# Two borders and one tick order: a long convolution with a spectral mix, its stages between batch pairs put in another order

## The chip, the cores and the metric

The kernel runs on one core of a Trainium2 chip. The metric is the device time of one execution in microseconds (us). TensorE (PE) multiplies matrices into the accumulator memory PSUM, VectorE (DVE) and ScalarE (ACT) copy results out of PSUM into the on-chip memory SBUF and do the elementwise work, GpSimd (POOL) and SyncE (SP) here mostly issue DMA transfers. Each engine works through its own list of instructions in order, and engines wait for one another by semaphores.

## The reference

An input x of 8 batches, 5696 positions and 128 channels is convolved causally with a filter h of 5696 positions, by Fourier transforms of twice the length. The result goes through a spectral mix of its lowest 64 modes and a small dense layer:

```python
Yf = np.fft.rfft(x, n=L, axis=1) * np.fft.rfft(h, n=L, axis=0)[None]   # L = 2 * S
v = np.fft.irfft(Yf, n=L, axis=1)[:, :S, :]
X = np.fft.rfft(v, axis=1)                          # modes 0..63 are mixed
Yr = einsum(Xr, w_r) - einsum(Xi, w_i)              # 'bmd,mde->bme'
Yi = einsum(Xr, w_i) + einsum(Xi, w_r)
u = v + np.fft.irfft(Y, n=S, axis=1)                # Y is zero above mode 63
out = u + np.maximum(u @ w_ch, 0.0)
```

## The kernel before

The 5696 positions are split as 89 times 64. The batches are worked on in four pairs (`for g_ in range(NP)`, L682), numbered 0 to 3 here. For each pair there are two parts.

The first transform runs over the 89. `a_tile(j, slots, eng)` (L438) makes one of 32 tiles of it: four matmuls of 180 columns with constant `F` (in SBUF `Xin` holds the pair's input), into a slot of two PSUM banks, and one eviction to `As` with a scale, on ACT or DVE. Tile 31 is evicted in two halves, one on each engine ("both"). Slots are named by their first bank: 0, 2, 4, 6.

Then come 23 ticks (`NT`), one for each group of four of the 90 frequencies (the last has two). In tick t of a pair, `tick(g_, t)` (L612) issues:

- the placing of a piece of the next pair's input into `Xin` on DVE, in eight of the ticks (`x_place`, L355, by the list `XPLACE`);
- the second transform of group t (`second`, L568): 16 matmuls whose operands `As` and `M` have 64 rows, into slot 0 or 2;
- its product with the filter's spectrum (`products`, L579): ACT copies the slot to `Xs`, DVE multiplies `Xs` with `Hs` into `U`;
- a load of the next pair's input by POOL (`x_load`);
- the third transform of group t - 2 (L634 to L649): two halves of two matmuls of 512 columns on `U`, each into one of the banks 4, 5, 6 in turn, evicted by ACT to `Zs` (or `Zt`), then written to DRAM (`zscr`) by a DMA that SP issues;
- the mode sums of group t - 3 (L655 to L668): eight matmuls of `Zs` with `G`, all added up in bank 7 over the whole pair;
- in ticks 0 to 16 of pair 0 only, a filter group (`filter_tick`, L455): 16 matmuls of 64 rows on `Ah` into banks 2 and 3, evicted by DVE to `Hs`, and two DMAs by SP that copy it across partitions. It is for the product six ticks later.

In the pairs 1 to 3, two second transforms are issued together in every other tick. In pair 0, while there is filter work, second transforms have only slot 0. There the kernel before issues second(t + 1) already in tick t, from tick 2 on, between the third transform and the mode sums:

```python
if g_ == 0 and LC <= t < NT - 1:
    second(g_, t + 1)
```

As third transform and mode sums lag by two and three ticks, ticks 23 to 25 only finish them. After the last pair they run as they are; after pairs 0, 1 and 2 the first six tiles of the next pair's first transform are put among them by a list `border` (L521) of tile, slot and engine:

```python
border = {NT - 1: [(0, 0, V)], NT: [(1, 2, V), (2, 0, V)],
          NT + 1: [(3, 2, A), (4, 0, V)], NT + 2: [(5, 2, V)]}
```

Then ACT copies the mode sums out of bank 7 (to `XT`), and the other 26 tiles follow in four slots, on ACT and DVE in turn with two on ACT in a row every ninth (L696). `keep(n, b0)` (L537) issues n matmuls of constants into banks b0 and b0 + 1 whose results nobody reads. In the borders POOL also issues pieces of a rewriting of the mixing weights to DRAM, one after every other tile.

After the four pairs come the mix of the modes, the inverse transform from `zscr`, the dense layer and the output; the change does not touch them.

`share(n)` (L428) chooses between ACT and DVE for an eviction: it adds a given cost to each engine's running sum and takes the smaller. The kernel before uses it for the first pair's first transform only.

Of the kernel before, what the change touches and what calls it, by code (L numbers as in the profile page):

```python
# [123 lines left out]
def bass_long_conv_fft__then__afno_spectral_mix_kernel(nc, x, h, moe_w_r, moe_w_i, moe_w_ch, out):  # L124
# [8 lines left out]
    NP = B // 2  # L133
# [103 lines left out]
    XC = 4  # L237
# [117 lines left out]
    def x_place(i, src, toks):  # L355
        R.add("vector", lambda e: e.tensor_copy(bass.AP(x_sb, i * XN * XS, [[XW, NQ], [XS, XN], [1, D]]),  # L356
                                                bass.AP(src, 0, [[XB, NQ], [D, XN], [1, D]])),
              list(toks) + XZ, [("xin", i)])
# [159 lines left out]
            [("s4", part, 0)], after=pace + (AST if part else M_ALL[1:4]))  # L518

    V, A = "vector", "scalar"  # L520
    border = {NT - 1: [(0, 0, V)], NT: [(1, 2, V), (2, 0, V)], NT + 1: [(3, 2, A), (4, 0, V)], NT + 2: [(5, 2, V)]}  # L521
    early = {0: lambda: load_id(), 1: lambda: load_w(0), 3: lambda: load_w(1), 6: lambda: load_w(2), 8: lambda: load_w(3),
             12: lambda: load_s4(1), 16: lambda: load_s4(0),
             14: lambda: clear_zt(0),
# [20 lines left out]
    def with_h_at(g_, t):  # L545
        return g_ == 0 and t + LH < NT
# [10 lines left out]
    def twin(g_, t):  # L557
        return g_ > 0 and t % 2 == 1

    def straight(g_, t):  # L560
        return g_ > 0 and t % 4 == 3
# [6 lines left out]
    def second(g_, t):  # L568
        sl = slot_of(g_, t)
        for i, k in enumerate(ticks[t]):  # L570
            for r in range(2):
                for b in range(2):
                    col = k * 3 * J + (J if r == 0 else 0) + b * J
                    mm(pv(sl + b, i * D, [[1, D]]),
                       ap(m_sb, MW, J * b, J, col, [[1, P]]),
                       ap(a_sb, AW, J * b, J, (2 * k + r) * D, [[1, D]]), r == 0, r == 1,
                       AST + mtok(k), [bank(sl + b)])

    def products(g_, t, sl):  # L579
        n = len(ticks[t])  # L580
        bk = [bank(sl), bank(sl + 1)]
        i = t % NU
        hv = bass.AP(h_sb, KT * t * D, [[2 * HW, P], [HW, 2], [0, 2], [1, n * D]])
        uv = bass.AP(u_s[i], 0, [[2048, P], [1024, 2], [512, 2], [1, n * D]])
        src = pv(sl, 0, [[0, 2], [512, 2], [1, n * D]])
        if t == 0:
            e = turns("e", list(range(NXS)))
            evac(bass.AP(x_s[e], 512, [[1024, P], [1, n * D]]), pv(sl + 1, 0, [[1, n * D]]), [bank(sl + 1)], [("xs", e)], eng="scalar")
            hv = bass.AP(h_sb, 0, [[2 * HW, P], [HW, 2], [1, n * D]])
            for b, s_, tok, done in ((0, pv(sl, 0, [[0, 2], [1, n * D]]), bank(sl), ("u", i)),  # L590
                                     (1, bass.AP(x_s[e], 512, [[1024, P], [0, 2], [1, n * D]]), ("xs", e), ("u0", i))):
                R.add("vector", lambda e, b=b, s_=s_: e.tensor_tensor(bass.AP(u_s[i], b * 512, [[2048, P], [1024, 2], [1, n * D]]), s_, hv, MULT),  # L592
                      [tok, ("h", t, 0), ("h", t, 1, 0), ("h", t, 1, J)], [done])
            return
        if not straight(g_, t):
            e = onchip.get((g_, t))
            if e is None:
                e = copied(g_, t, sl)
            src, bk = bass.AP(x_s[e], 0, [[1024, P], [0, 2], [512, 2], [1, n * D]]), [("xs", e)]
        R.add("vector", lambda e: e.tensor_tensor(uv, src, hv, MULT),  # L600
              bk + [("h", t, 0), ("h", t, 1, 0), ("h", t, 1, J)], [("u", i)])
# [7 lines left out]
    def xtok(n):  # L609
        return [("xt", n, p_) for p_ in range(2)]  # L610

    def tick(g_, t):  # L612
        if g_ + 1 < NP:
            for i in range(2 * XC):
                if t == XPLACE[g_ > 0][i]:
                    x_place(i, x_st[i], xtok(i))
        with_h = with_h_at(g_, t)
        if t < NT:
            of_two = t > 0 and twin(g_, t - 1)
            if not of_two and not (g_ == 0 and t > LC):  # L620
                second(g_, t)
            products(g_, t, slot_of(g_, t))
            if twin(g_, t):
                second(g_, t + 1)
                if straight(g_, t):
                    copied(g_, t + 1, slot_of(g_, t + 1))
        drain = list(border[t]) if t in border and g_ + 1 < NP else []
        if drain and t >= NT:
            j, sl, e = drain.pop(0)
            a_tile(j, [sl], e)  # L630
        if g_ + 1 < NP and t % 2 == 0 and 0 < t <= 4 * XC:
            i = t // 2 - 1
            x_load(g_ + 1, i, x_st[i], xtok(i), [("u", t % NU)] + AST)
        if LC <= t < NT + LC:  # L634
            s_ = t - LC
            n = len(ticks[s_])
            i, zi = s_ % NU, zroom(g_, s_)
            zb = [turns("z", ZBANK) for b in range(2)]
            for b in range(2):
                for r in range(2):  # L640
                    mm(pv(zb[b], 0, [[1, n * D]]), (W1, W2)[r], u_s[i][:, r * 1024 + b * 512:r * 1024 + b * 512 + n * D],
                       r == 0, r == 1, [("u", i), ("wc",)] + ([("u0", i)] if s_ == 0 and b else []), [bank(zb[b])])
                evac(bass.AP(z_s[zi], b * D, [[1024, P], [2 * D, n], [1, D]]),
                     pv(zb[b], 0, [[D, n], [1, D]]), [bank(zb[b])], [("zs", zi, b)], eng="scalar",
                     after=once(("zx", zi, b), Z_OLD) if zi >= NZ else ())
            zo = (g_ * NK + KT * s_) * P * 256
            dma("sync", bass.AP(zs, zo, [[256, P], [P * 256, n], [1, 256]]),
                bass.AP(z_s[zi], 0, [[1024, P], [256, n], [1, 256]]), "z",
                [("zs", zi, 0), ("zs", zi, 1)], [("zd", g_, s_)])  # L649
            if drain and t >= NT:  # L650
                j, sl, e = drain.pop(0)
                a_tile(j, [sl], e)
        if g_ == 0 and LC <= t < NT - 1:
            second(g_, t + 1)
        if LM <= t < NT + LM:  # L655
            s_ = t - LM
            zi = zroom(g_, s_)
            for b in range(2):
                for i, k in sorted(enumerate(ticks[s_]), key=lambda q: (s_ > 0 or q[1] != 1, q)):
                    if k % 2:  # L660
                        o, off, n, sl = pv(MB, b * P, [[1, P]]), (k + 1) // 2 * P, P, (k + 1) // 2
                    else:
                        ms, off = even[k]
                        n, sl = 2 * len(ms), 0
                        dims = [[M, 2]] if len(ms) == 1 else [[ms[1] - ms[0], 2], [M, 2]]
                        o = pv(MB, b * P + ms[0], dims)
                    mm(o, z_s[zi][:, i * 256 + b * P:i * 256 + b * P + P], g_sb[:, off:off + n],
                       k == 1 and b == 0, k == NK - 1 and b == 1, [("g", sl // GP), ("zs", zi, b)], [bank(MB)])  # L668
        if drain and t < NT + LM - 1:
            j, sl, e = drain.pop(0)  # L670
            a_tile(j, [sl], e)
        if with_h:
            filter_tick(t + LH, [2, 3])

# [5 lines left out]
            filter_tick((j - 11) // 3, [b_, b_ + 1], share(512))  # L680
    keep(12, turns("s", SLOTS))
    for g_ in range(NP):  # L682
        for t in range(NT + LM):
            tick(g_, t)
            if g_ == 0 and t < 2:
                keep(8, 4)
            assert g_ + 1 < NP or not wp
            if g_ == NP - 1 and t in early:
                pace[:] = [("u", min(t, NT - 1) % NU)]
                early[t]()  # L690
        evac(bass.AP(xt, 2 * g_ * XTW + M, [[B * XTW, P], [XTW, 2], [1, P]]), pv(MB, 0, [[P, 2], [1, P]]),
             [bank(MB)], [("xt", g_)], 1.0 / 64, eng="scalar", after=[("ag", k) for k in range(NS + 2 * XN, NK)])
        evac(bass.AP(xt, 2 * g_ * XTW, [[B * XTW, P], [XTW, 2], [1, M]]), pv(MB, M, [[P, 2], [1, M]]),
             [bank(MB)], [("xtn", g_)], -1.0 / 64, eng="vector" if g_ + 1 == NP else "scalar", after=[("ag", k) for k in range(NS + 2 * XN, NK)])
        if g_ + 1 < NP:
            for j in range(6, 32):  # L696
                a_tile(j, [(4, 6, 0, 2)[(j - 7) % 4] if j > 6 else 0], "both" if j == 31 else (A, V)[(j - 6) % 9 % 2])
                if j == 31:
                    keep(8, 6)
                if wp and j % 2 == 1:  # L700
                    dst, src_, ring, tok = wp.pop(0)
                    dma("gpsimd", dst, src_, ring, (), [tok], after=[("as", j)])
# [189 lines left out]
```

## Time and profile before

| | us |
|---|---|
| median of three runs | 386.07 (385.49 to 386.13) |
| the profiled execution | 385.34 |
| its span | 383.2 |
| pair 0: ticks, from the first second transform to pair 1's | 43.88 to 109.12 |
| pair 1 to pair 2's first second transform | 109.12 to 164.28 |
| pair 2 to pair 3's first second transform | 164.28 to 219.06 |
| PE busy of 53.12 in pair 0's ticks (43.88 to 97.00) | 51.97 |
| ACT, DVE busy there | 44.68, 45.17 |

Times in the trace count from the span's start. A row of the timeline has start, length, engine, line, operation, what is written from what is read, and how many instructions were merged; the brackets give the engine's idle time before it and who ended that. A matmul's end is modelled, its start is recorded, so that PE groups are best read from start to start. PEld is the loading of weights. In the profile the third transform is `ps<-U,Wc`, the second `ps<-As,M`, the mode sums `ps<-G,Zs`, the filter `ps<-Ah,M` and the first transform `ps<-F,Xin`.

### The profile page before, as it was taken

How to read it: one execution, taken by the hardware profiler on the slowest of the kernel's cores; microseconds unless marked ns; L12 is line 12 of the kernel's file. 1: busy time of each engine (PE TensorE's matmuls, PEld its weight loads, DVE VectorE, ACT ScalarE, POOL GpSimd, SP SyncE). 2: the span in 40 equal slices, each digit the busy share in tenths (PEclk: the TensorE clock that was granted, in tenths of full speed). 3: DMA queues.
4: the chain of work that ended last, by engine and by line, in shares of the span. 5: the costliest groups of instructions: out<-in, count | busy, mean ns of one | idle time of the engine just before them, and what ended most of it. 6: DMA issues, size and time to landing. Idle time of an engine off the chain costs nothing.

```text
span 383.2 us, 12588 instructions
## 1 busy us (share of the span) xinstructions
PE 366.0 (96%) x5392; PEld 283.7 (74%) x5392; DVE 310.5 (81%) x348; ACT 302.7 (79%) x488; POOL 82.5 (22%) x133
## 2 busy tenths in 40 slices
PE   7999899999989999989999999999999999999994
PEld 7998756666866666866667866668898988887873
DVE  6969888998888999998998888875447767776876
ACT  1359688898889997989997999995457676776785
POOL 8400022220552320733310411319200000000000
PEclk9999999999999999999999999997999999999999
DMA  7998469999699997999995859999999999999879
GB/s 149 194 283 339 138 125 291 273 244 261 96 138 210 226 249 220 101 133 204 263 257 164 87 167 370 334 327 388 402 402 398 414 405 406 412 405 378 359 279 356
DMA packets 86865, 103.94 MB, mean 271 GB/s; under 512 B 22638, under 2 KB 72430, under 8 KB 83330
## 3 DMA queue, kind: packets, MB, share of 16 engines
q1 hardware_dynamic: 62523, 67.73, 50.5%
q0 software_dynamic: 24288, 35.43, 44.1%
q8 instruction: 42, 0.69, 0.7%
q14 instruction: 12, 0.10, 0.1%
HBM read 70.61 MB, written 51.12 MB: 318 GB/s over the span
## 4 chain that ended last, share of the span: by engine, by line
PE 69%; ACT 10%; DMA 9%; DVE 6%; POOL 2%; issue 2%; SPq 0%; DVEq 0%; POOLq 0%
PE ps L320 69%; ACT As L310 6%; DMA Xr<-in_x_dram 4%; DMA ZT0b<-zscr 4%; POOL Xr L317 2%; DVE As L314 2%; DVE U L592 1%; ACT UT L308 1%; ACT R L826 1%; ACT Zt L308 1%; DVE Xin L356 1%; ACT Xs L308 1%; DVE U L600 1%; DVE O L827 1%; DVE UT L312 0%
## 5 line engine op out<-in xcount | busy, mean ns | idle before, releaser
L600 DVE TENSOR_TENSOR U<-Xs,Hs 128x2048 f16<-128x2048 f16 (+1 forms) x73 | 86.7, 1190 | 12.0 <-ACT Xs L308 10.4
L320 PE MATMUL ps<-U,Wc 128*128 128x512 f16 (+1 forms) x368 | 94.0, 376 | 0.0
L308 ACT CAST Xs<-ps 128x1024 f16<-128x1024 f32 (+1 forms) x77 | 75.0, 979 | 9.0 <-PE ps L320 7.4
L308 ACT CAST Zs<-ps 128x512 f16<-128x512 f32 (+1 forms) x134 | 70.6, 596 | 5.9 <-PE ps L320 5.8
L827 DVE TENSOR_TENSOR O<-ps,R 128x512 f32<-128x512 f32 x81 | 52.6, 686 | 20.5 <-ACT R L826 15.2
L826 ACT ACTIVATE R<-ps 128x512 f32<-128x512 f32 x96 | 51.0, 573 | 14.2 <-PE ps L320 13.7
L314 DVE TENSOR_SCALAR As<-ps 128x720 f16<-128x720 f32 (+1 forms) x64 | 53.2, 880 | 5.1 <-PE ps L320 3.4
L320 PE MATMUL ps<-F,Xin 128*128 128x180 f16 x512 | 52.3, 250 | 2.6 <-DVE Xin L356 1.2
L320 PE MATMUL ps<-As,M 64*128 64x128 f16 x1440 | 50.6, 217 | 4.2 <-DVE U L592 3.0
L320 PEld LDWEIGHTS ps<-As,M 64*128 64x128 f16 x1440 | 40.3, 94 | 17.9 <-issue 8.1
L310 ACT ACTIVATE As<-ps 128x720 f16<-128x720 f32 x68 | 48.0, 768 | 6.4 <-PE ps L320 5.6
L320 PE MATMUL ps<-WI,UT 128*128 128x256 f16 x360 | 52.0, 279 | 0.5 <-DVE O L827 0.4
L320 PEld LDWEIGHTS ps<-F,Xin 128*128 128x128 f16 x512 | 44.5, 155 | 9.5 <-DVE As L314 2.6
L320 PEld LDWEIGHTS ps<-U,Wc 128*128 128x128 f16 x368 | 28.7, 97 | 27.6 <-ACT Zs L308 4.4
L317 POOL DMA_DIRECT2D Xt<-in_x_dram x48 | 26.0, 545 | 104.6 <-PE ps L320 100.2
L308 ACT CAST UT<-ps 128x712 f16<-128x712 f32 x40 | 30.0, 752 | 18.8 <-PE ps L320 17.8
L320 PEld LDWEIGHTS ps<-WI,UT 128*128 128x128 f16 x360 | 39.3, 152 | 4.4 <-issue 2.1
L320 PE MATMUL ps<-IBs,C 128*128 128x356 f16 x128 | 40.1, 323 | 0.6
L320 PEld LDWEIGHTS ps<-G,Zs 128*128 128x128 f16 x524 | 27.4, 96 | 11.7
L600 DVE TENSOR_TENSOR U<-ps,Hs 128x2048 f16<-128x2048 f32 x15 | 34.3, 2284 | 0.0
L320 PE MATMUL ps<-G,Zs 128*128 128x128 f16 (+2 forms) x524 | 32.6, 192 | 0.0
L320 PE MATMUL ps<-F 128*128 128x180 f16 x280 | 27.7, 254 | 2.5 <-DMA F<-cF 2.5
(86 smaller groups left out, 506.1 us busy)
## 6 DMA issues: line engine op xcount, KB each, us to landing
out_dram<-O SPq DMA_DIRECT2D x39, 512.0 KB, 11.4
zscr<-Zs SPq DMA_DIRECT2D x64, 256.0 KB, 6.8
Xt<-in_x_dram POOLq DMA_DIRECT2D x24, 320.0 KB, 7.0
zscr<-Zt SPq DMA_DIRECT2D x24, 256.0 KB, 6.6
W<-wscr POOLq DMA_DIRECT2D x4, 1024.0 KB, 8.9
M<-cM POOLq DMA_DIRECT2D x5, 720.0 KB, 20.5
ZT0a<-zscr SPq DMA_DIRECT2D x3, 1024.0 KB, 14.0
Hs<-Hs SPq DMA_DIRECT2D x44, 64.0 KB, 5.8
```

The costliest lines, as they stand in the source:

```text
L308: R.add(e, lambda h_: h_.copy(dst, src), reads, writes, after=after)
L310: R.add(e, lambda h_: h_.activation(dst, src, COPY, scale=scale), reads, writes, after=after)
L314: R.add(e, lambda h_: h_.tensor_scalar_mul(dst, src, scale), reads, writes, after=after)
L317: R.add(eng, lambda h_: h_.dma_start(dst, src), reads, writes, ring=ring, after=after)
L320: R.add("tensor", lambda h_: h_.matmul(o, l, r, start=st, stop=sp), reads, writes)
L356: R.add("vector", lambda e: e.tensor_copy(bass.AP(x_sb, i * XN * XS, [[XW, NQ], [XS, XN], [1, D]]), bass.AP(src, 0, [[XB, NQ], [D, XN], [1 ...
L592: R.add("vector", lambda e, b=b, s_=s_: e.tensor_tensor(bass.AP(u_s[i], b * 512, [[2048, P], [1024, 2], [1, n * D]]), s_, hv, MULT), [tok, ...
L600: R.add("vector", lambda e: e.tensor_tensor(uv, src, hv, MULT), bk + [("h", t, 0), ("h", t, 1, 0), ("h", t, 1, J)], [("u", i)])
L826: R.add("scalar", lambda e: e.activation(rv, src_r, RELU), bk, [("r", i % NR)], after=once(("r", i % NR), G_ALL + XTT + [("y", 0), ("y", 1 ...
L827: R.add("vector", lambda e: e.tensor_tensor(ov, src_u, rv, ADD), bk + [("r", i % NR)], [key + (h_,)], after=once(key, old))
```

## The change

Three things are changed. The third transform and the mode sums become functions of their own, `third(g_, s_)` and `modes_of(g_, s_)`. In pair 0 the second transform of tick t is issued at the start of tick t, in all ticks. And after pairs 0, 1 and 2 the ticks end with the 23rd; what is left of the third transforms is issued first, tiles 0 and 1 between the two, then tiles 2, 3 and 4 between the mode sums, in the slots 0, 2 and 4. Engines of the tiles are chosen by `share` with starting sums. Tiles from 5 on take the slots 0, 4, 6, 2 in turn (before, from 7 on, 4, 6, 0, 2), so that the last tile is in slot 6 and the constant matmuls go to banks 2 and 3.

```diff
-    border = {NT - 1: [(0, 0, V)], NT: [(1, 2, V), (2, 0, V)], NT + 1: [(3, 2, A), (4, 0, V)], NT + 2: [(5, 2, V)]}
...
+    def third(g_, s_):
+        if 0 <= s_ < NT:
...
+    def modes_of(g_, s_):
+        if 0 <= s_ < NT:
...
-            if not of_two and not (g_ == 0 and t > LC):
+            if not of_two:
                 second(g_, t)
...
-        if g_ == 0 and LC <= t < NT - 1:
-            second(g_, t + 1)
...
+        third(g_, t - LC)
+        modes_of(g_, t - LM)
         if with_h:
             filter_tick(t + LH, [2, 3])
...
-        for t in range(NT + LM):
+        for t in range(NT + LM if g_ + 1 == NP else NT):
...
+        if g_ + 1 < NP:
+            load.update(scalar=600.0, vector=0.0)
+            third(g_, NT - 2)
+            a_tile(0, [0], share(720))
+            a_tile(1, [2], share(720))
+            third(g_, NT - 1)
+            load["scalar"] += 560.0
+            a_tile(2, [0], share(720))
+            modes_of(g_, NT - 3)
+            a_tile(3, [4], share(720))
+            modes_of(g_, NT - 2)
+            a_tile(4, [2], share(720))
+            modes_of(g_, NT - 1)
+            load["scalar"] += 700.0
...
-            for j in range(6, 32):
-                a_tile(j, [(4, 6, 0, 2)[(j - 7) % 4] if j > 6 else 0], "both" if j == 31 else (A, V)[(j - 6) % 9 % 2])
+            for j in range(5, 32):
+                a_tile(j, [(0, 4, 6, 2)[(j - 5) % 4]], "both" if j == 31 else share(720))
                 if j == 31:
-                    keep(8, 6)
+                    keep(8, 2)
```

By `share`, tiles 0, 2, 3 and 5 are evicted by DVE and 1 and 4 by ACT (before: 0, 1, 2, 4, 5 by DVE and 3 by ACT); the tiles from 6 on have the engines that they had.

More of the change, by code (lines that the diff above doesn't have):

```diff
@@ L610, in xtok @@
         return [("xt", n, p_) for p_ in range(2)]
[L612 to L619, printed above, removed]
-            if not of_two and not (g_ == 0 and t > LC):
-                second(g_, t)
-            products(g_, t, slot_of(g_, t))
-            if twin(g_, t):
-                second(g_, t + 1)
[L625 to L635, printed above, removed]
+    def third(g_, s_):
+        if 0 <= s_ < NT:
             n = len(ticks[s_])
@@ L649, in tick @@
                 [("zs", zi, 0), ("zs", zi, 1)], [("zd", g_, s_)])
-            if drain and t >= NT:
-                j, sl, e = drain.pop(0)
-                a_tile(j, [sl], e)
-        if g_ == 0 and LC <= t < NT - 1:
-            second(g_, t + 1)
-        if LM <= t < NT + LM:
-            s_ = t - LM
+    def modes_of(g_, s_):
+        if 0 <= s_ < NT:
             zi = zroom(g_, s_)
@@ L668, in tick @@
                        k == 1 and b == 0, k == NK - 1 and b == 1, [("g", sl // GP), ("zs", zi, b)], [bank(MB)])
-        if drain and t < NT + LM - 1:
-            j, sl, e = drain.pop(0)
-            a_tile(j, [sl], e)
+    def tick(g_, t):
+        if g_ + 1 < NP:
+            for i in range(2 * XC):
+                if t == XPLACE[g_ > 0][i]:
+                    x_place(i, x_st[i], xtok(i))
+        with_h = with_h_at(g_, t)
+        if t < NT:
+            of_two = t > 0 and twin(g_, t - 1)
+            if not of_two:
+                second(g_, t)
+            products(g_, t, slot_of(g_, t))
+            if twin(g_, t):
+                second(g_, t + 1)
+                if straight(g_, t):
+                    copied(g_, t + 1, slot_of(g_, t + 1))
+        if g_ + 1 < NP and t % 2 == 0 and 0 < t <= 4 * XC:
+            i = t // 2 - 1
+            x_load(g_ + 1, i, x_st[i], xtok(i), [("u", t % NU)] + AST)
+        third(g_, t - LC)
+        modes_of(g_, t - LM)
         if with_h:
@@ L690, in bass_long_conv_fft__then__afno_spectral_mix_kernel @@
                 early[t]()
+        if g_ + 1 < NP:
+            load.update(scalar=600.0, vector=0.0)
[11 more added lines that the diff above has]
+            load["scalar"] += 700.0
         evac(bass.AP(xt, 2 * g_ * XTW + M, [[B * XTW, P], [XTW, 2], [1, P]]), pv(MB, 0, [[P, 2], [1, P]]),
```

## The prediction

> **What bounds the kernel now.** I read the page's busy table first, then the chain of waits in order of time, then the timeline of TensorE (PE) in one tick of the first pair, of ScalarE (ACT) and VectorE (DVE) there, and of a border between pairs.
>
> The page, then the chain (start, length, engine):
>
> ```profile
> PE 366.0 (96%) x5392; PEld 283.7 (74%) x5392; DVE 310.5 (81%) x348; ACT 302.7 (79%) x488; POOL 82.5 (22%) x133
> ```
>
> ```profile
> 51.71 45.05 PE ps L320 x784
> ...
> 101.58 7.49 ACT As L310 x11
> ```
>
> The ticks of pair 0 are one unbroken piece of PE, so there every PE microsecond counts; in a border the evacuations of the first transform are the chain.
>
> PE, one tick of pair 0 with filter work, and groups elsewhere:
>
> ```profile
> 59.91 1.04 PE L320 MATMUL ps<-U,Wc 128*128 128x512 f16 x4
> 60.88 0.62 PE L320 MATMUL ps<-As,M 64*128 64x128 f16 x16
> 61.43 0.50 PE L320 MATMUL ps<-G,Zs 128*128 128x2 f16 x8
> 61.86 0.41 PE L320 MATMUL ps<-Ah,M 64*128 64x64 f16 x16
> 62.20 1.04 PE L320 MATMUL ps<-U,Wc 128*128 128x512 f16 x4
> ```
>
> ```profile
> 48.08 0.62 PE L320 MATMUL ps<-As,M 64*128 64x128 f16 x16
> 48.64 1.04 PE L320 MATMUL ps<-U,Wc 128*128 128x512 f16 x4
> 49.81 0.62 PE L320 MATMUL ps<-As,M 64*128 64x128 f16 x16
> 50.27 0.40 PE L320 MATMUL ps<-Ah,M 64*128 64x64 f16 x16
> ```
>
> ```profile
> 113.58 1.04 PE L320 MATMUL ps<-U,Wc 128*128 128x512 f16 x4
> 114.45 0.49 PE L320 MATMUL ps<-G,Zs 128*128 128x128 f16 x8
> ```
>
> Read from start to start: a group's price depends on what follows it. U (third transform) costs 0.97 before As (second transform, 64-row operands), but 0.87 before G (mode sums). As costs 0.55 or 0.56 before a 128-row group, but 0.46 before Ah (filter, also 64-row). Going in or out of 64-row work thus costs about 0.10 each time. A tick of pair 0 has the order U, As, G, Ah: it goes in twice and out twice, 0.97 + 0.55 + 0.43 + 0.34 = 2.29.
>
> ACT and DVE beside it, and ACT and DVE in the border after pair 1:
>
> ```profile
> 61.54 1.01 ACT L308 CAST Xs<-ps 128x1024 f16<-128x1024 f32 x1
> 62.85 1.07 ACT L308 CAST Zs<-ps 128x512 f16<-128x512 f32 x2 [0.29 <-PE ps L320]
> ```
>
> ```profile
> 149.50 1.07 ACT L308 CAST Zs<-ps 128x512 f16<-128x512 f32 x2 [1.24 <-PE ps L320]
> 151.11 0.78 ACT L310 ACTIVATE As<-ps 128x720 f16<-128x720 f32 x1 [0.54 <-PE ps L320]
> 151.78 0.64 ACT L308 CAST Zs<-ps 128x256 f16<-128x256 f32 x2
> 152.77 0.55 ACT L310 ACTIVATE XT<-ps 128x256 f16<-128x256 f32 x2 [0.35 <-PE ps L320]
> 153.47 1.45 ACT L310 ACTIVATE As<-ps 128x720 f16<-128x720 f32 x2
> ```
>
> ```profile
> 154.87 9.15 DVE L314 TENSOR_SCALAR As<-ps 128x720 f16<-128x720 f32 x11 [0.19 <-PE ps L320]
> 155.18 9.04 ACT L310 ACTIVATE As<-ps 128x720 f16<-128x720 f32 x13 [0.27 <-PE ps L320]
> ```
>
> ACT starts its border with 2.55 us of idle (1.24 + 0.54 + 0.35 in brackets, 0.15 before the row of 153.47, and 0.27). From tile 9 on DVE runs to 164.02 and ACT, from tile 10, to 164.22; pair 2 starts at 164.28.
>
> **The change, part by part.**
>
> *1. Pair 0's order.* No instruction is added; second(t) moves from behind the third transform of tick t-1 to the start of tick t. PE's cycle becomes As, U, G, Ah: As before U 0.55, U before G 0.87, G before Ah 0.43, Ah before As x. x has no row. Its ends: Ah before U, 0.34, less the 0.10 for going out gives 0.24; a group that pays for going in, as G before Ah, gives 0.43. I take 0.24, by the nearest row, As before Ah, which pays neither (0.46 against 0.55). Tick: 2.09 against 2.29. The Trainium skill, TensorEngine Tiling, Key Properties, says that changing the tiling mode drains TensorE while another tile of the same mode does not; by it Ah to As, both 64-row with 128 columns of weights, is free and x is the low end. If every change of group drained, x would be 0.43 and the tick 2.28: the rows of As before Ah speak against that.
>
> What could stop the shorter tick: ACT needs 0.93 + 0.99 = about 1.9 a tick (its starts while it runs without idle: 84.36, 86.22, 88.08). DVE needs 1.15 for the product and 0.61 for the filter's eviction, and 0.60 more in the ticks 9, 10, 12, 15, 16 that place the next input. In the new order the eviction of filter(t) stands behind the product, and filter(t+1) needs its banks: second 0.67, copy 1.01, product 1.15, eviction 0.69, with 0.12 of handing over, is 3.64 after the tick's start; filter(t+1) is due at 2.09 + 1.85 = 3.94. Two placings in a row use that up: I charge 0.2 in all. SP's list is the same in order: 2 x 0.60 + 0.59 of issuing a tick without G loads, under 2.09. Filter lands 6 ticks before its product (12.4 us; landing 6.1 median, 8.2 at most), and rooms of Zs come round after 6 ticks too (12.5 against 6.8), so queues keep their cover. Input loads by POOL wait for the product of their tick and land in 4.4 to 7.7, six ticks ahead.
>
> Start: now third(1) and second(4) wait behind copies (second(3) only at 49.81, second(4) at 51.71), and third(2) starts at 53.03. New: second(2) 48.08, third(0) 48.64, filter 49.61, second(3) 49.85, third(1) 50.40, modes 51.27, filter 51.70, second(4) 51.94, third(2) 52.49: 0.54 earlier. Then twelve ticks to third(14): 12 x 0.20 = 2.44; less the 0.2; one half tick, 2.18 to 1.97, 0.21. PE is 0.54 + 2.44 - 0.2 + 0.21 = 3.0 ahead at third(15). Ticks 17 to 21 have no filter: 0.55 + 0.87 + 0.42 = 1.84 as before, and ACT, at 1.86, runs full.
>
> *2. End of pair 0.* Now second(22) comes a group later and its copy stands before Zs(20) on ACT. Followed through in the same way: Zs(20) starts 89.79 (was 92.38), third(21) 89.88, its second half waits for Zs(20) to 90.42, tile 0 on PE 90.86, As0 on DVE 91.43, As1 on ACT 91.87, Zs(22) to 93.20, tile 3 (banks 4 and 5, behind Zs(22)) 93.25, As4 93.95 on PE and 94.53 on ACT, XT to 95.78, tile 7 (bank 7, behind XT) 95.83, As9 on DVE 97.23, As10 on ACT 97.40. Now they are 99.73 and 100.04. With the same runs of 9.15 and 9.03 (ACT's in this border) the next pair's operands are complete and the border ends at 106.43, and pair 1 starts 106.5 instead of 109.12: 2.6 of the 3.0 is left.
>
> *3. Borders after pairs 1 and 2.* Third transforms are the same four groups, ahead of tiles that they used to follow; of the tiles, 1 and 4 go from DVE to ACT and 3 from ACT to DVE, the later ones keep their engines. ACT has one tile more, 0.70, and DVE one less. Pair 1 worked through: third(21) PE 147.64 (was 148.86); tile 0 148.51 (148.18), As0 149.08; tile 1 148.81, As1 on ACT behind Zs(21), 149.40; third(22) 149.19, Zs(22) on ACT 150.10 to 150.74; tile 2 in As0's slot 150.05, As2 150.63; modes; tile 3 waits for Zs(22), 150.79, As3 151.46; modes; tile 4 151.49, As4 on ACT 152.07; modes, XT 152.77 to 153.32; tile 5 152.07, As5 152.64; tile 6 152.43, As6 153.30; tile 7 behind XT 153.37, As7 153.94; As8 154.25, As9 154.77, As10 154.95. Behind tile 3's wait stand modes(21), tile 4 and XT, and ACT is idle for 1.37 there, in place of three idles. The run starts 0.10 earlier on DVE and 0.23 on ACT; the later end moves from 164.22 to 163.99: 0.2, twice.
>
> *4. Small ones.* The eight constant matmuls go to banks 2 and 3 because tile 31 moves to 6 and 7; both before and after they follow tile 28's eviction: 0. POOL issues 14, 14 and 4 weight pieces in the borders, for 13, 13, 6: one more of 0.74, beside POOL's idle; if that cover went, 0.8 at most. Moved write-backs by SP start up to 1.2 earlier; nobody waits for them before the last stage: 0.
>
> *Sum:* -2.6 - 0.2 - 0.2 = -3.0. The profiled execution took 385.34 (span 383.2, 2.1 around it), so 382.3 there; that execution was 0.73 below the median 386.07, so 383.1 against the median. The later pairs and the last stage are paced by PE and move as a block.
>
> **The rivals.**
>
> *A. Half the tick's saving.* Ah to As costs 0.34 (as Ah to U) instead of 0.24, or ACT, whose queue has only about 0.1 us left a tick in the new order (Zs ends 0.09 before the next copy is ready), holds PE. Each takes 0.1 x 12 = 1.2: -1.8, 384.3. For: x has no row, and ACT runs full one tick kind later. Against: As before Ah, and ACT's need of 1.86. The Trainium skill, TensorEngine Tiling, PSUM Bottleneck, says that packing tiles speeds up TensorE but not the copies out of PSUM, which may then bind; by it the tick can't go under ACT's 1.86, which the sum doesn't reach.
>
> *B. No measurable change:* x is 0.43, which leaves 0.01 a tick; the start's 0.54 is eaten by the 0.4 of pair 0's end and the 0.2 of DVE. Only the borders' 0.4 stays: -0.3, 385.8.
>
> *C. Slower, by tile 3's wait.* It stands at the head of PE's queue, in banks 4 and 5, until ACT has gone through Zs(21), As1 and Zs(22). If that lasts longer than I have it, all that is behind (two mode groups, tiles 4 to 8, XT and so bank 7) moves with it. At 1.0 us more per border, 3.0 in all, the gain is gone; at 1.5 us, 1.5 slower: 387.6. For: ACT's FIFO has three evictions of 0.6 to 1.1 in front. Against: their durations have rows, and an error of 1.0 is more than any one of them but Zs(21).
>
> *D. The transfers bind:* pair 0 moves 227 GB/s, the DMA share is 0.92 there, and a tick shorter by 9% asks for 9% more. The last stage moves 386, so I give it no time of its own; it would look like A.
>
> **How the numbers follow.** Forecast 383.1 (382.0 to 384.0: borders wrong by 0.3 each), chance 0.55. A 0.21, B 0.10, C 0.14. About 0.2%, 0.77 us, is what a measurement of this kernel can tell from no change, so under 385.3 is faster: forecast and A, 0.76; B 0.10; C 0.14. Range: down to 381.9 (border tiles 0.4 each better), up to 385.9 so that A and B are inside and only C and a little below are out.
>
> **What would show it.** In the changed profile: U to U in pair 0's filter ticks 2.09 (A: 2.19 or more; B: 2.28); no gap in PE there but short ones near ticks 10 and 11 behind the filter's eviction; pair 1's first product near 107 instead of 109.8; one ACT idle of about 1.4 per border, and, in pairs 1 and 2, 16.0 from the start of the last product to the next pair's second transform, in place of 16.24 (148.04 to 164.28). The prediction is wrong if PE has waits for ACT in pair 0's ticks, or if tile 9 starts later than 7.5 us after the last product of pairs 1 and 2 (6.7 by the list above).

## The result, and the profile after

The changed kernel takes 383.56 us (median of 20 executions, 382.0 to 385.79), the kernel before, run beside it on the same chip, 386.0 (20 executions). The ratio is 0.9948 [0.9931, 0.9964]: about 2.0 us faster, 1.4 to 2.7 by the interval (2.4 between the medians). The forecast was 3.0 faster, 383.1.

Execution by execution the changed kernel differs by 3.8 us, and the one that was profiled is its slowest, 385.79 (span 383.7). It is therefore read together with a second profiled execution of the same kernel (label after_again, 384.83, span 382.7). The stages, from one pair's first second transform to the next one's:

| | start of pair 0 | pair 0 | pair 1 | pair 2 | start of pair 3 |
|---|---|---|---|---|---|
| before | 43.88 | 65.24 | 55.16 | 54.78 | 219.06 |
| changed, first profile | 44.18 | 65.66 | 54.39 | 54.44 | 218.67 |
| changed, second profile | 43.94 | 65.12 | 54.41 | 54.77 | 218.24 |
| by the prediction | 43.88 | 62.6 | 55.0 | 54.6 | 216.1 |

Pair 0, which was to give 2.6, gave nothing. Pair 1 gave 0.75, where 0.2 was forecast. What follows pair 3's start is not touched by the change; it took 164.2, 165.0 and 164.5, so that a span alone, with 0.9 of chance in its last part, could not show this.

The page's busy table of the changed kernel, first profile:

```profile
PE 363.0 (95%) x5392; PEld 284.2 (74%) x5392; DVE 309.0 (81%) x345; ACT 304.2 (79%) x491; POOL 82.2 (21%) x133
```

PE has the same 5392 instructions and 3.0 us less of busy time: it does its work in less, and the span does not follow. In the chain of waits (start, length, what), pair 0's ticks were one piece of 45.05 us before. Now they are broken. The first profile's chain has a PE gap that nothing in the profile explains, a write-back and a product; the second profile's has copies of the filter in the same place:

```profile
60.69 0.92 issue
61.61 6.36 PE ps L320 x128
...
78.65 7.96 DMA zscr<-Zs
...
91.17 1.24 DVE U L599
```

```profile
73.33 6.34 DMA Hs<-Hs
...
82.94 7.26 DMA Hs<-Hs
...
90.39 1.24 DVE U L599
```

A tick of PE in pair 0, first profile, where nothing holds it:

```profile
52.78 1.04 PE L320 MATMUL ps<-U,Wc 128*128 128x512 f16 x4
53.65 0.49 PE L320 MATMUL ps<-G,Zs 128*128 128x2 f16 x8
54.07 0.41 PE L320 MATMUL ps<-Ah,M 64*128 64x64 f16 x16
54.31 0.61 PE L320 MATMUL ps<-As,M 64*128 64x128 f16 x16
54.86 1.04 PE L320 MATMUL ps<-U,Wc 128*128 128x512 f16 x4
```

From start to start: 0.87 + 0.42 + 0.24 + 0.55 = 2.08. The tick is as short as the prediction had it, and the disputed step, filter to second transform, is 0.24.

The border after pair 1, ACT and DVE, first profile:

```profile
147.85 2.10 ACT L308 CAST Zs<-ps 128x512 f16<-128x512 f32 x4
...
152.34 0.79 ACT L310 ACTIVATE As<-ps 128x720 f16<-128x720 f32 x1 [1.17 <-PE ps L320]
...
153.43 10.75 ACT L310 ACTIVATE As<-ps 128x720 f16<-128x720 f32 x15
```

```profile
154.03 9.96 DVE L314 TENSOR_SCALAR As<-ps 128x720 f16<-128x720 f32 x12 [0.29 <-PE ps L320]
```

One ACT idle of 1.17 is left of the former 2.55, and from 153.43 (ACT) and 154.03 (DVE) both run without a stop to their ends at 164.2 and 164.0.

### The profile page after: what moved, and what is told of

The parts are those of the page before. It is cut to its first block, busy times and chain, and to the rows that moved or that the text cites. A ratio compares the mean times of both kernels' runs of the same rounds, so it can differ in the third digit from the quotient of the medians.

```text
span 383.7 us, 12576 instructions
## 1 busy us (share of the span) xinstructions
PE 363.0 (95%) x5392; PEld 284.2 (74%) x5392; DVE 309.0 (81%) x345; ACT 304.2 (79%) x491; POOL 82.2 (21%) x133
## 4 chain that ended last, share of the span: by engine, by line
PE 66%; DMA 11%; ACT 10%; POOL 5%; DVE 5%; issue 2%; POOLq 0%; DVEq 0%; ACTq 0%
PE ps L320 66%; ACT As L310 6%; DMA Xr<-in_x_dram 5%; DMA ZT4b<-zscr 4%; DMA zscr<-Zs 2%; POOL Xr L317 2%; DVE As L314 2%; DVE U L591 1%; ACT R L831 1%; ACT UT L308 1%; POOL ZT3b L501 0%; POOL ZT1b L501 0%; POOL ZT2b L501 0%; DVE UT L312 0%; ACT Xs L308 0%
## 5 line engine op out<-in xcount | busy, mean ns | idle before, releaser
L308 ACT CAST Xs<-ps 128x1024 f16<-128x1024 f32 (+1 forms) x77 | 74.8, 975 | 12.4 <-PE ps L320 8.9
L310 ACT ACTIVATE As<-ps 128x720 f16<-128x720 f32 (+1 forms) x71 | 50.8, 771 | 8.0 <-PE ps L320 7.1
L314 DVE TENSOR_SCALAR As<-ps 128x720 f16<-128x720 f32 (+1 forms) x61 | 50.7, 879 | 6.2 <-PE ps L320 4.7
L320 PEld LDWEIGHTS ps<-G,Zs 128*128 128x128 f16 x524 | 28.8, 96 | 14.0
L312 DVE CAST UT<-ps 128x712 f16<-128x712 f32 x24 | 21.4, 890 | 11.2 <-PE ps L320 11.2
## 6 DMA issues: line engine op xcount, KB each, us to landing
ZT0a<-zscr SPq DMA_DIRECT2D x3, 1024.0 KB, 13.3
```

The costliest lines, as they stand in the source:

```text
L308: R.add(e, lambda h_: h_.copy(dst, src), reads, writes, after=after)
L310: R.add(e, lambda h_: h_.activation(dst, src, COPY, scale=scale), reads, writes, after=after)
L312: R.add(e, lambda h_: h_.tensor_copy(dst, src), reads, writes, after=after)
L314: R.add(e, lambda h_: h_.tensor_scalar_mul(dst, src, scale), reads, writes, after=after)
L320: R.add("tensor", lambda h_: h_.matmul(o, l, r, start=st, stop=sp), reads, writes)
```

## The experiments

Ratios are to the kernel before in the same job, with 95% intervals; a ratio of 0.9900 is 3.9 us. The lengths of pair 0 are from the one profiled execution of each kernel.

### Which part gives what

The changed kernel was run again, and each half of the change alone. **order_only** is the kernel before with pair 0's new order:

```diff
-            if not of_two and not (g_ == 0 and t > LC):
+            if not of_two:
                 second(g_, t)
...
-        if g_ == 0 and LC <= t < NT - 1:
-            second(g_, t + 1)
```

**border_only** is the changed kernel with those lines put back, so that only the borders are new.

> The changed kernel once more, for a second profile of it. Theory 1 (pair 0's new order gives about 2.6 us, the borders after pairs 1 and 2 about 0.3 each, and the stalls of the first changed profile in pair 0 are chance of that execution): pair 0's ticks at 2.08 us without PE gaps, pair 1 starting at most 63.0 us after pair 0's first second transform (65.24 before), total 2.5 to 3.0 us under the kernel before. Theory 2 (the shorter tick of 2.08 outruns the transfers, so that write-backs and filter copies land late in every execution): gaps behind landings between 60 and 95 us again, pair 0 over 64 us, total 1.5 to 2.5 under.

> Only the first pair's second transforms at the start of their ticks; the borders as before. Theory 1: 2.5 to 3.0 us under the kernel before, as much as the whole change. Theory 2: pair 0's gain is mostly eaten by late transfers, 0.5 to 1.5 us under.

> Only the borders as in the changed kernel; pair 0's second transforms one group ahead as before. Theory 1: each border gains 0.2 to 0.35 us, 0.6 to 1.0 us under the kernel before. Theory 2 (the borders carry the change): 1.5 us under or more.

Measured: after_again 0.9977 [0.9939, 1.0015] (384.97, six executions); order_only 0.9993 [0.9963, 1.0023] (385.78); border_only 0.9964 [0.9939, 0.9989] (384.69). Pair 0 took 65.12, 65.68 and 65.21. The borders alone give about 1.4 us; the order alone gives nothing that can be measured, and with the borders it adds nothing that these runs can tell. So the larger step of the prediction was lost inside pair 0.

Where it was lost, the second profile of the changed kernel shows. Two of VectorE's products (`U<-Xs,Hs`) between 81 and 93 us:

```profile
85.82 1.23 DVE L599 TENSOR_TENSOR U<-Xs,Hs 128x2048 f16<-128x2048 f16 x1 [1.99 <-DMA Hs<-Hs]
...
90.39 2.36 DVE L599 TENSOR_TENSOR U<-Xs,Hs 128x2048 f16<-128x2048 f16 x2 [1.29 <-DMA Hs<-Hs]
```

With two more of 0.19 and 0.23, products wait 3.7 us in all for the copies of the filter across partitions, which SP issues. The first profile has the same waits, under other names:

```profile
91.17 2.36 DVE L599 TENSOR_TENSOR U<-Xs,Hs 128x2048 f16<-128x2048 f16 x2 [2.17 <-ACT Zt L308]
```

This product needs no `Zt`, and its own copy `Xs` was done at 88.67. Its two filter copies landed at 90.76 and 90.98, 0.19 before it starts, just as 90.20 stands 0.19 before 90.39 in the second profile. Two more products start 0.19 after a landing, after 1.01 and 0.87 of waiting: 4.05 in all.

What PE lost by it, second profile, then first:

```profile
87.11 1.04 PE L320 MATMUL ps<-U,Wc 128*128 128x512 f16 x4 [0.92 <-DVE U L599]
...
91.67 1.04 PE L320 MATMUL ps<-U,Wc 128*128 128x512 f16 x4 [1.03 <-DVE U L599]
```

```profile
92.45 1.04 PE L320 MATMUL ps<-U,Wc 128*128 128x512 f16 x4 [1.97 <-DVE U L599]
```

That is 1.95 and 1.97 behind late products. PE also stops for 0.76 (0.64 and 0.12) and 1.04 (0.92 and 0.12) where no wait is shown (last section). Taken off pair 0, the two leave 62.4 and 62.65, where 62.6 was worked out (an estimate: what would bind next is not in these rows). So about two thirds of the loss are the late copies, and one third are stops whose cause is open.

SP's own list, first of the kernel before, then of the changed kernel (second profile); the last filter group was evicted from 83.04 and from 81.40:

```profile
82.85 1.68 SPq L317 DMA_DIRECT2D Hs<-Hs  x2
84.57 0.61 SPq L317 DMA_DIRECT2D zscr<-Zs  x1
85.27 1.86 SPq L317 DMA_DIRECT2D Hs<-Hs  x2
```

```profile
84.61 1.28 SPq L317 DMA_DIRECT2D Hs<-Hs  x2
85.94 0.69 SPq L317 DMA_DIRECT2D zscr<-Zs  x1
86.73 1.23 SPq L317 DMA_DIRECT2D Hs<-Hs  x2
```

From 56 us on, SP issues three DMAs a tick with one pause over 0.1 us in each of the two lists (0.44 and 0.43). Before, the copies of group 8 were issued at 51.71 and those of group 22 at 85.27: 33.56 / 14 = 2.40 a group, against evictions every 2.29. But the lag from the start of an eviction to the issue of its copies did not grow evenly: it is 0.72 to 0.94 in the groups 8 to 11, 1.78 and 2.57 in the next two, and then 2.1 to 2.8 to the end. From group 13 to 22 SP took (85.27 - 64.88) / 9 = 2.27 a group, so it just kept up with the old tick. In the changed kernel it is 51.85 to 86.73, 2.49 a group, against evictions every 2.17; the lag is 0.86 at group 8, 3.65 at group 12 and 5.33 at group 22, and over the last ten groups SP took 2.41 a group against evictions every 2.24. The wait of 1.29 is for group 20: evicted from 76.73, its second copy issued at 82.94 and landed 7.26 later, at 90.20.

**rooms** asked whether the rooms of `Zs` for write-backs, which are six up to pair 0's group 11 and ten from then on, were the cause. With it group 12 goes on to the seventh room, where it began again with the first:

```diff
-        return (s_ - 2 * NZ) % NZX if g_ == 0 and s_ >= 2 * NZ else s_ % NZS[g_]
+        return (s_ - NZ) % NZX if g_ == 0 and s_ >= 2 * NZ else s_ % NZS[g_]
```

> The changed kernel, and in pair 0 third transforms 12 to 15 go to the four late rooms Zt, so that a room of Zs is written again after 10 ticks, not 6, from third transform 12 on. Theory 1: no difference from the changed kernel, within 0.4 us. Theory 2 with the write-backs as the late transfer: 0.5 to 1.5 us under the changed kernel, and no ACT wait on a write-back in pair 0.

Measured: 0.9959 [0.9931, 0.9988] (384.2), pair 0 64.79. No row of ACT in its pair 0 waits for a write-back, but its chain of waits still has a filter copy of 7.00, and two products wait 2.84 and 0.71 until 0.19 after a copy's landing. More rooms alone don't bring the gain back.

### Taking the late transfers away

Three kernels take the suspected cause away in different places. **lead7** makes each filter group one tick earlier, **hs_pool** lets POOL issue the filter's copies and leaves SP the write-backs, and **one_x** loads only the first of the next pair's input pieces in pair 0 and places it eight times, so that the transfers have less to move (pair 1 then works on other input than its own).

```diff
-    LC, LM, LH = 2, 3, 6
+    LC, LM, LH = 2, 3, 7
```

```diff
-            dma("sync", ..., "s", [("h", t, 0)], [("h", t, 1, p0)])
+            dma("gpsimd" if t >= LH else "sync", ..., "h" if t >= LH else "s", [("h", t, 0)], [("h", t, 1, p0)])
```

```diff
-                    x_place(i, x_st[i], xtok(i))
+                    n_ = i if g_ else 0
+                    x_place(i, x_st[n_], xtok(n_))
...
-        if g_ + 1 < NP and t % 2 == 0 and 0 < t <= 4 * XC:
+        if g_ + 1 < NP and t % 2 == 0 and 0 < t <= (4 * XC if g_ else 2):
```

> The changed kernel with the filter groups seven ticks ahead of their product instead of six (one group more among the first pair's first transform, one less in the ticks). Theory 2a (the changed kernel's pair 0 waits because filter copies, issued 1 to 2 us after their eviction and landing 8 to 9 us later, now come after their product is ready): no DVE wait on a filter copy after 80 us, pair 0 from first to first second transform about 63.5 us instead of 65.1 to 65.7, total 1 to 2 us under the changed kernel. Theory 2b (the landings only grow with the load, whatever the lead): waits stay. For the gap of PE near 60.5 us, in the middle of a filter group after its 14th matmul: if it is the fetch of instructions in blocks of 128 matmuls with their weight loads, it stands 16 matmuls earlier in the work, after the 6th mode sum of that tick.

> The changed kernel with the filter copies of the ticks issued by POOL instead of SP, so that they neither wait in SP's list behind write-backs nor stand in the same queue. Theory 2a with SP's list and queue as the delay: landings of filter copies fall from 6.4 to about 3 us, no waits on them, 1 to 2 us under the changed kernel. If the delay is the load on the DMA engines as such: landings stay at 6 to 9 us and the total stays within 0.5 us. POOL issues two transfers more per tick, 1.1 us, and its input loads are queued among them.

> The changed kernel with seven of the eight input loads in pair 0's ticks left out; each placing copies the first piece, so that pair 1 computes on wrong input and all engines do the same work. 2.5 MB less of 12.2 MB that move in pair 0. Theory 2 (the load on the transfers makes the landings late): landings under 6 us in the median, no waits on filter copies and none on PE's instructions, pair 0 at 63 us or less, total 2 to 2.5 us under the changed kernel. Theory 1 (no transfer is to blame): within 0.5 us of the changed kernel.

> The changed kernel with seven ticks of lead for the filter and with the late rooms for write-backs. If write-back rooms bind once the filter copies do not: 0.3 to 1 us under the kernel with the lead alone. If not: the same as it.

| | ratio | median | pair 0 | copy of filter, issue to landing (median, longest) |
|---|---|---|---|---|
| changed, second profile | 0.9977 [0.9939, 1.0015] | 384.97 | 65.12 | 6.4, 9.1 |
| lead7 | 0.9948 [0.9924, 0.9971] | 383.52 | 63.66 | 5.8, 8.1 |
| hs_pool | 0.9904 [0.9872, 0.9935] | 382.07 | 63.66 | 6.2, 7.8 |
| one_x | 0.9890 [0.9866, 0.9914] | 381.91 | 63.11 | 3.3, 7.2 |
| rooms_lead7 | 0.9927 [0.9902, 0.9953] | 383.18 | 63.65 | 6.4, 8.1 |

lead7, hs_pool and one_x each end the waits for filter copies, in their own way, and pair 0 is 1.46, 1.46 and 2.0 us shorter than in the second profile. Not all of that is theirs: lead7 and hs_pool are also without the PE stop of 0.64, while one_x has one of 0.71. hs_pool tells most: with POOL the copies land about as long after their issue as before, 6.2 against 6.4 (the fall to about 3 that was expected did not come), and yet nobody waits for them. What had been late was the issue, in SP's list. POOL in that kernel, with the eviction of group 22 at 82.25:

```profile
84.50 1.07 POOL L317 DMA_DIRECT2D Hs<-Hs  x2
```

That is 2.25 behind the eviction, where the changed kernel has 5.33. The Trainium skill, DMA: Bandwidth & Descriptors, Issuing engine by pattern, holds the path by SyncE to be generally the faster one, and that by GpSimd the more flexible. Here the path by GpSimd is as fast to land (6.2 against 6.4 us), and the kernel is faster with it, since SyncE's list is full. lead7 has the same pair 0 in its profile and a median 1.45 higher; its twelve executions lie between 382.2 and 386.5, those of hs_pool between 381.0 and 384.6, and what sets them apart was not traced.

one_x shows the same from the side of the load. Busy time by stretch, of the changed kernel (second profile) and of one_x (columns: stretch and its length, then PE, PEld, DVE, ACT, POOL busy with instruction counts, granted clock, DMA share, GB/s; the DMA share adds up the times of packets and can pass 1):

```profile
68.00:76.00 8.00, 8.00 (x172) 5.40 (x168) 7.71 (x10) 7.43 (x12) 2.07 (x4) 1.00 1.07 256
84.00:92.00 8.00, 6.05 (x92) 3.74 (x85) 4.66 (x5) 6.64 (x12) 0.00 (x0) 1.00 1.09 286
```

```profile
68.00:76.00 8.00, 7.90 (x162) 5.23 (x158) 7.74 (x10) 7.47 (x12) 0.00 (x0) 1.00 0.58 162
84.00:92.00 8.00, 8.00 (x111) 4.89 (x107) 6.49 (x7) 8.00 (x15) 0.00 (x0) 1.00 0.72 211
```

With the DMA share down from 1.07 and 1.09 to 0.58 and 0.72, PE has no idle in the second stretch, where it had 1.95. Pair 0 is 63.11, of which 0.71 is one PE gap of the unexplained kind (below): 62.4 without it, against 62.6 worked out. SP is not much quicker there: it takes 2.30 a group (51.93 to 84.13) and ends 2.6 behind the last eviction. What one_x adds is that the copies then land in 3.3 in the median.

lead7 and hs_pool keep one wait each. In lead7 the second transform of tick 16 goes into banks that the last filter group has just filled; in hs_pool ACT has no room to write `Zs` to, since a write-back is late (landing of the write-backs 7.0 in the median, 13.3 at most):

```profile
79.04 0.62 PE L320 MATMUL ps<-As,M 64*128 64x128 f16 x16 [1.44 <-DVE Hs L312]
```

```profile
72.52 1.07 ACT L308 CAST Zs<-ps 128x512 f16<-128x512 f32 x2 [1.55 <-DMA zscr<-Zs]
```

### The two left waits, and the old order

**lead7_slot** gives the second transforms after the filter's end the other slot, so that tick 16 does not meet the last filter group. **before_lead7** does the same two edits on the kernel before. **lead7_pool** is lead7_slot and hs_pool in one, **pool_rooms** is hs_pool and rooms.

```diff
-            return XSLOT[(t + 1) % 2 if t and not with_h_at(g_, t) else 0]
+            return XSLOT[t % 2 if t and not with_h_at(g_, t) else 0]
```

> The changed kernel with the filter seven ticks ahead, and the alternation of pair 0's two slots turned round after the last filter tick, so that second(16) does not go to banks 2 and 3, which the last filter group has just filled (the one wait of 1.44 us in the kernel with the lead alone). Theory 2a (filter copies with no cover ate the gain): pair 0 62.2 us (63.67 less 1.44), which is what the prediction's working gave without late transfers (62.6), total 3.5 to 4 us under the kernel before. If another transfer is next: a new wait in pair 0, 63 us or more.

> The kernel before with the same lead of seven ticks and the same slots: old order of pair 0, old borders. Its ticks are bound by PE at 2.29 us and no copy was late, so the lead by itself should give little: one filter tick of 0.3 to 0.4 us moved out of the ticks into the first transform, pair 0 64.6 to 65.2 us, total within 0.8 us of the kernel before. If it gives 2 us, then the lead and not the order is what the last kernel gains.

> The changed kernel with filter copies issued by POOL and the late rooms for write-backs. With POOL alone, the one wait left in pair 0 was for a write-back (ACT held at 73 us, PE 0.63, a landing of 13.3 us). Theory 2: that wait goes, pair 0 63.0 us, total 0.5 us under the kernel with POOL alone. Otherwise the same as it.

> The seven-tick lead with its slots and the filter copies issued by POOL, together. If the lead alone takes all waits on filter copies away, nothing more to gain: within 0.4 us of the kernel with lead and slots. If SP's list also holds up write-backs: 0.5 us better, pair 0 62 us or less.

| | ratio | median | pair 0 |
|---|---|---|---|
| lead7_slot | 0.9926 [0.9894, 0.9958] | 383.1 | 63.63 |
| before_lead7 | 0.9991 [0.9965, 1.0018] | 385.58 | 65.04 |
| pool_rooms | 0.9902 [0.9865, 0.9938] | 382.38 | 62.90 |
| lead7_pool | 0.9892 [0.9857, 0.9928] | 382.29 | 62.87 |

In lead7_slot the wait of 1.44 is gone, and pair 0 is not shorter, because a wait for a write-back stands in its place:

```profile
85.96 1.07 ACT L308 CAST Zs<-ps 128x512 f16<-128x512 f32 x2 [1.51 <-DMA zscr<-Zs]
```

With POOL issuing as well, that one goes too; PE's longest gap in pair 0 from 50 us on is then 0.65, behind ACT (lead7_pool), and an unexplained 0.39 (pool_rooms), and pair 0 takes 62.87 and 62.90, 0.3 above the working. before_lead7 shows that a longer lead is worth nothing in the old order (0.9991): there the tick of 2.29 was the bound, and the copies were in time.

lead7_pool has the lowest ratio of the kernels that do the whole work, 4.2 us (1.08%) under the kernel before, or 3.4 between the medians; its six executions lie within 381.07 and 382.51. By their intervals hs_pool and pool_rooms can't be told from it.

## Why the prediction was right in its sum and wrong in its parts

- *Tick of PE, x = 0.24: right.* 2.08 measured, 2.09 worked out (12 x 0.20 is 2.40, though, where the sum has 2.44), and the low end of x that was taken is the measured value. The Trainium skill, TensorEngine Tiling, Key Properties, names a drain only for a change of tiling mode, and the trace agrees: 0.24 from 64-row filter to 64-row second transform, against 0.34 from the filter to the 128-row third transform before.
- *Start 0.54 earlier: right.* From pair 0's first second transform to third(2) it is 8.60 (52.78 less 44.18), before 9.15.
- *0.2 for DVE in two placings in a row: right in size.* The third transforms of one_x there start at 66.06, 68.14 and 70.39: one tick of 2.25 in place of 2.08, so 0.17.
- *"SP's list is the same in order: 2 x 0.60 + 0.59 ..., under 2.09": the step that failed.* The issue durations were taken as 0.6 each. The rows of the kernel before, in the later ticks, have 1.68 and 1.86 for two copies and 0.6 for the write-back, and SP took 2.27 a tick there, all of the old tick of 2.29 and more than 2.09. That was in the trace and was not read: the view of one early tick, with a lag of 0.8, does not show the 2.1 to 2.8 of the later ones. In the changed kernel the lag grows by 0.32 a group in the mean, (5.33 - 0.86) / 14.
- *"Filter lands 6 ticks before its product (12.4 us; landing 6.1 median)": failed with it.* The lead was counted from the filter's matmuls to the product, without the eviction, without SP's lag, and with 2.08 for the last ticks too, which have no filter and take 1.85. With 4 to 5 us of lag and landings of 6.4 in the median, 9.1 at most, nothing of the lead is left.
- *End of pair 0: -2.6.* Right as a working where the transfers are out of the way: pair 1 begins at 107.21 in one_x and 106.92 in lead7_pool, against 106.5 worked out. In the changed kernel it begins at 109.84 and 109.06, before at 109.12, and so the sign that was named for this step, pair 1's first product near 107, did not come (110.51 and 109.72).
- *Borders after pairs 1 and 2, -0.2 each: right in kind, too small.* From the start of the third transform of group 20 to the next pair's first second transform it is 17.40 for 17.84 (pair 1) and 17.32 for 17.79 (pair 2), in the first profile: -0.44 and -0.47. ACT's one idle is 1.17 where 1.37 was worked out, and the working had gaps of 0.47 (DVE) and 0.25 (ACT) between tiles 5 and 8, where DVE in fact waits 0.29 and ACT runs on. From the start of the last product to the second transform, pair 1 has 15.84 (164.23 less 148.39); 16.0 was forecast for 16.24. Pair 1 gained another 0.3 in its ticks before, which was not traced further. One wait that the working did not name fits where the borders gained. In the old border after pair 1, PE's first tile waits for the last placing of the next input:

```profile
148.18 0.85 PE L320 MATMUL ps<-F,Xin 128*128 128x180 f16 x8 [0.38 <-DVE Xin L356]
```

After pair 2 it waits 0.35, and after pair 0 it does not wait. The new borders have no such wait, since a third transform stands in that place, and take 17.3 to 17.4 after pairs 1 and 2 in every run that has them, about what the old one after pair 0 took (17.37); the old ones take 17.8 to 18.1 in before, order_only and before_lead7, each with such a wait of 0.35 to 0.66. No run takes this wait away alone.
- *Border after pair 0, +0.4: wrong.* It was to cost 0.4; measured in the same way it takes 17.39 (border_only 17.34), before 17.37. Where no copies are late (lead7, hs_pool, one_x) it is 17.48 to 17.59, so 0.1 to 0.2 of the 0.4 are there.
- *Small ones at 0:* no wait in these traces contradicts them.
- *The rivals.* A and B put the loss into x or ACT, C into tile 3's wait; none of these showed. It was D, the transfers, which was named and got neither a time nor a chance of its own, on the ground that the last stage moves 386 GB/s. That compared bytes. What ran full was the issuing of many small transfers by one engine, and a stage with larger ones says nothing about that. Nor did it look like A, as was said of it: the tick stayed at 2.08, and the loss came as gaps.
- *The signs:* the two that were to prove the prediction wrong did not come. No PE wait in pair 0's ticks is for ACT, and tile 9 starts 6.5 and 6.3 after the last products of pairs 1 and 2 (154.86 less 148.39, 209.29 less 202.95). But "no gap in PE there", a sign of being right, failed in both profiles.

So the 383.1 came out near 383.56 by luck, by two errors against each other: 2.6 expected and not had in pair 0, and 0.4 expected and about 1.4 had in the borders, by border_only. Even so, the 3.0 lies outside the interval of 1.4 to 2.7. The profiles show 0.75 of the 1.4 in pair 1 and 0.38 in pair 2 (54.40 in lead7, hs_pool and lead7_pool; in border_only it is 54.82, with a late input load in its chain). That is 1.1, well inside the 0.4 to 2.4 of border_only's interval, so nothing need be missing. Whether the changed kernel's 2.0 holds some gain of pair 0 in most executions, which its two profiles don't show, is open too: the intervals of 0.9948 and 0.9964 overlap.

## What to carry to other kernels

Before a tick is made shorter, each DMA queue's issues per tick must be compared with the new tick, with the durations that they have in the busiest ticks, and the lag from producer to issue be read over the whole stage: where it is well above that of the first ticks and the engine issues without a pause, the queue has no slack for a shorter tick. The cover of a transfer runs from the end of its producer's eviction to its consumer, less the lag in the list of the issuing engine. Groups with the same operand rows should stand together on PE, and an idle engine such as POOL can take over a share of the issues.

## What had not been expected of the hardware

- The issue of one small DMA by SP takes 0.46 to 0.62 us around 50 us, and from 80 to 88 us, with the DMA share at 1.08 to 1.09, 0.36 to 0.82 for a write-back and 1.23 to 1.95 for two copies; POOL takes 1.07 for two in hs_pool. That the load stretches SP's issue is shown only in small part: one_x, with far less load, still needs 2.30 a group for 2.49. What else does is open.
- Landing follows the load: a copy of 64 KB lands in 3.3 us in the median in one_x, whose DMA share from 60 to 92 us is 0.58 to 0.91, and in 5.8 to 6.8 in all other kernels, with 0.96 to 1.12.
- PE stops in the middle of a group of 16 matmuls with nothing to wait for. First profile of the changed kernel, the 14 matmuls before the gap and the 2 after it:

```profile
60.31 0.38 PE L320 MATMUL ps<-Ah,M 64*128 64x64 f16 x14
61.61 0.20 PE L320 MATMUL ps<-Ah,M 64*128 64x64 f16 x2 [0.92 <-issue]
```

The gap is 0.64 in the second profile, 0.99 in order_only, 0.52 in rooms, 0.71 in one_x and 0.39, at another place, in pool_rooms. The kernel before, before_lead7, border_only, lead7, rooms_lead7, lead7_slot and lead7_pool have none over 0.1 in pair 0. A second gap follows 128 matmuls after the first: 0.39 in order_only, and 0.12 in rooms and in both profiles of the changed kernel; hs_pool has only one of 0.12, at 67.12. The page lists a queue of instructions with 42 packets and 0.69 MB, 16.4 KB each, which is 64 bytes for each of 256 PE instructions, matmuls and weight loads, if those are what it carries. A fetch of instructions that comes late would fit both; a gap that was to move with lead7 did not show there, and nothing here tests it. Its cause is open.
